# Shift of the exponentials by pairwise sums, the order of all instructions computed anew, and early loads into other places: an attention and MLP kernel

## The chip, the cores and the metric

The kernel runs on one core of a Trainium2 chip. The metric is the device time of one execution in microseconds (us). The five engines named below are PE (TensorE, the matrix engine), DVE (VectorE), ACT (ScalarE), POOL (GpSimd) and SP (SyncE, which here only issues DMAs). Each runs its own instructions strictly in its own order; between engines there are semaphores.

## The reference, cut to what matters

Random-feature attention for 8 batches of 8 heads (576 rows of 64), then a two-layer MLP over the 4608 tokens:

```
proj = x_s @ omega.T                      # x_s: q or k, scaled
h = proj - sum(x_s * x_s) / 2
phi = exp(h - max(h)) / sqrt(128)         # for q and for k
num = phi_q @ (phi_k.T @ v);  den = phi_q . sum(phi_k) + 1e-6
x = (num / den) as (4608, 512)
out = (silu-gate(x @ w_in)) @ w_out       # g = h * sigmoid(h)
```

So every row has one shift, `-(max - sq) - sq`, that is added to its 128 projections before the exponential.

## The kernel before, in words

Two heads make a pair; there are 32 pairs. Of a pair, PE projects k and q (`project`, L405, 16 small matmuls with 64 rows, and `project_mid`, L412, for the middle tile), DVE takes the row maxima from PSUM (`top`, L419 and L421), ACT squares k and q in their natural layout (`square`, L378), and DVE sums the squares (`square_sum`, L382). DVE then makes the shift in `shift` with two small instructions, a `tensor_tensor` (L425) and a `scalar_tensor_tensor` (L426), both with two operands in SBUF. ACT takes the exponentials (L441, or after an addition on DVE, L446 and L449, all at once in L455). PE sums the exponentials of k (L476 and L478 in the first eight pairs, later POOL adds them first, L461 to L466, and PE finishes, L470) and multiplies them with v (L499). DVE makes the denominators (`denom`, L487, ten products with a read each, and a reciprocal, L492), POOL scales with them (`normal`, L517), PE transposes (`turn`, L523), ACT copies (L535), PE multiplies (`numer`, L561). ACT and DVE split the result into a high and a low part (L580 and L585), which are the MLP's operand x.

The MLP runs as float32 in three passes over such high and low parts, with 512-column matmuls. The first 3 of 9 token tiles are done directly (`stage1` L736, `silu` L873 and L875, `g_low` L879, `stage2` L982); the other six in three pairs of tiles by a Strassen-like scheme: a first stage of products (L821, gathered by DVE on L868), and a second (L935, whose operands DVE prepares on L901 and L925). The weights are decoded from 64-bit words by ACT and DVE (L645, L659 to L665) and split by POOL (L678, L682); the first step of the MLP needs x of the first four pairs.

The order of all engines' instructions is computed in the kernel by a planner (`Plan.run`): a list of units of work, each with an engine, a duration, a due time (its key), predecessors, and places (rings of SBUF tiles and PSUM banks) that it takes and frees. The planner goes through the units by earliest possible start and then by key, and the kernel issues instructions in that order. `shift_keys` moves some keys by amounts drawn from the seeds in `SHIFTS`. Loads go on SP's queue in planned order. A load can be issued once its place is free: in the kernel before, `rawk`, `rawq`, `nat` and `v` are rings of two places each.

Of the kernel before, what the change touches and what calls it, by code (L numbers as in the profile page):

```python
# [19 lines left out]
P = 128  # L20
# [17 lines left out]
STRAIGHT_K = 22.298  # L38
STRAIGHT_Q = 25.574
# [3 lines left out]
WHOLE = ""  # L43
# [4 lines left out]
    "rawk": 2, "rawq": 2, "nat": 2, "v": 2, "sqk": 2, "sqq": 2, "hk": 2, "hq": 2,  # L48
# [6 lines left out]
for _f in range(16):  # L55
    RINGS[f"w{_f}"] = 1
PLAIN = 3
# [19 lines left out]
STAY = 19.283  # L77
HANDOFF = {"PE": 0.25, "ACT": 0.1, "DVE": 0.1, "POOL": 0.15, "SP": 0.2}
CALM = 0.5
SHIFTS = (  # L80
# [4 lines left out]
)  # L85
HOT = 100.0
PULSE = 0.24

# [10 lines left out]
PAIRS_22 = 52.068  # L99
PAIRS_28 = 85.000  # L100
# [6 lines left out]
PREPARE_2 = 0.176  # L107
LEAD_W = 14.593
# [49 lines left out]
def shift_keys(units):  # L158

    for seed in SHIFTS:  # L160
        r = random.Random(seed)
        part, wide = ((0.02, 6.0), (0.06, 3.0), (0.2, 1.5))[seed % 3]
        a, b = ((-20, 60), (40, 110), (100, 235), (200, 500), (420, 700), (640, 1100))[seed // 3 % 6]
        for u, d in [(u, r.gauss(0, wide)) for u in units if a <= u["key"] < b and r.random() < part]:
            u["key"] += d


class Plan:
# [6 lines left out]
    def add(self, name, eng, dur, key, fn, after=(), order=(), alloc=(), free=(), banks=0, table=None, lat=0.0, port=False, of="att", reads=()):  # L175
# [5 lines left out]
        self.units[name] = u  # L181
        for i in free:
            self.freed_by.setdefault(i, []).append(name)

    def run(self, until=None, heat=None):
        end, first = {}, {}
# [5 lines left out]
        table = None  # L192
# [10 lines left out]
        def slot_time(ring, back=0):  # L203
# [7 lines left out]
            for n in self.freed_by.get(s[i], ["never"]):  # L211
                if n not in end:
                    return None
                t = max(t, end[n] + HANDOFF[self.units[n]["eng"]])
            return t

        def bank_pools(u):
            pools = banks_of(u)
            chosen, when, used = [], 0.0, {p: 0 for p in pools}
            for _ in range(u["banks"]):  # L220
                best = None
                for p in pools:
                    t = slot_time(p, used[p])
                    if t is not None and (best is None or t < best[0]):
                        best = (t, p)
# [7 lines left out]
        while any(ready.values()):  # L233
            best = None
            for e, us in ready.items():
                pick, least = None, None
                for u in us:
                    t = 0.0
                    for a in u["after"]:
                        if self.units[a]["eng"] == e and not self.units[a]["lat"]:  # L240
                            t = max(t, end[a])
                        else:
                            t = max(t, first[a] + (CALM if e == "PE" and t > START_MLP else 0.0))
# [4 lines left out]
                    for j, (ring, _) in enumerate(u["alloc"]):  # L248
                        s = slot_time(ring, [r for r, _ in u["alloc"][:j]].count(ring))
# [12 lines left out]
                    t = max(t, free_at[e], port if u["port"] else 0.0)  # L262
                    key = u["key"]
                    if u["table"] and u["table"] != table:
                        key += STAY
                    least = t if least is None else min(least, t)
                    pick = (pick or []) + [(u, pools, key, t)]
                if not pick:
                    continue
                p = min((p for p in pick if p[3] <= least + 0.25), key=lambda p: p[2:])  # L270
# [6 lines left out]
            dur = u["dur"]  # L277
            if u["table"] and u["table"] != table:
                dur += SWITCH
                table = u["table"]  # L280
            if e == "PE":
                idle = t - free_at[e]
                u["hot"] = 0
                if u["banks"] and t < HOT and idle > 1.0:
                    since = max([free_at[e]] + [slot_time(p, pools[:i].count(p)) for i, p in enumerate(pools)])
                    u["hot"] = max(0, int((t - since - 0.4) / PULSE))
                    idle -= u["hot"] * PULSE
                if idle > 2.5:
                    warm = t + 4.0
                if t < warm:  # L290
                    dur *= 1.7
            free_at[e] = t + dur
            if u["port"]:
                port = t + dur
            done = t + dur
            if u["lat"]:
                pipe = max(pipe, t + dur + 1.0) + 0.75 * u["lat"]
                done = max(pipe + 0.25 * u["lat"], t + dur + 2.2)
            end[n] = done
            first[n] = done + HANDOFF[e]  # L300
            for i in u["reads"]:
                read[i] = e, first[n]
# [6 lines left out]
            if n == until:  # L309
                return t  # L310
# [9 lines left out]
def attention_mlp(ctx: ExitStack, tc: tile.TileContext, qT, kT, qn, kn, v, om_in, w_in, w_out, out, out_t):  # L320
# [43 lines left out]
    def load_raw(n, who):  # L364
        T["raw", n, who] = raw = new(f"raw{who}", [P, S + P])
        nc.sync.dma_start(raw, (kT if who == "k" else qT)[divmod(n, NPAIR)])

    def load_nat(n, who):
        T["nat", n, who] = nat = new("nat", [P, NC, D])
        nc.sync.dma_start(nat, (kn if who == "k" else qn)[divmod(n, NPAIR)])  # L370

    def load_v(n):
        T["v", n] = vt = new("v", [P, NC + 1, D])
# [5 lines left out]

    def square_sum(n, who):  # L380
# [3 lines left out]
    def raw_square(n, who):  # L384
        T["rsq", n, who] = sq = new({"k": "w12", "q": "w13"}[who], [P, S + P])
        nc.scalar.activation(sq, T["raw", n, who], AF.Square, scale=SCALE * 0.5**0.5)

    def mid_and_squares(n, who, ps):

        project_mid(n, who, ps)  # L390
# [1196 lines left out]
```

## Time and profile before

| | |
|---|---|
| three runs, us | 1018.7, 1022.9, 1023.67 (median 1022.9) |
| span of the profiled execution, us | 1018.3 (the page gives no other time of it) |
| busy: PE, DVE, ACT, POOL, us | 985.9, 779.8, 629.5, 362.0 |
| mean granted TensorE clock | 0.992 |
| chain that ended last | PE 73%, DVE 17%, DMA 4%, ACT 4% |

PE is busy for 97% of the span. Its matmuls are pipelined, so a busy PE isn't PE at its peak; start to start is the better measure of one. A group of instructions in the profile is named by line, engine, operation and tiles; what stands in square brackets in a timeline row is the idle time of the engine before the row and what ended it.

### The profile page before, as it was taken

How to read it: one execution, taken by the hardware profiler on the slowest of the kernel's cores; microseconds unless marked ns; L12 is line 12 of the kernel's file. 1: busy time of each engine (PE TensorE's matmuls, PEld its weight loads, DVE VectorE, ACT ScalarE, POOL GpSimd, SP SyncE). 2: the span in 40 equal slices, each digit the busy share in tenths (PEclk: the TensorE clock that was granted, in tenths of full speed). 3: DMA queues.
4: the chain of work that ended last, by engine and by line, in shares of the span. 5: the costliest groups of instructions: out<-in, count | busy, mean ns of one | idle time of the engine just before them, and what ended most of it. 6: DMA issues, size and time to landing. Idle time of an engine off the chain costs nothing.

```text
span 1018.3 us, 17380 instructions
## 1 busy us (share of the span) xinstructions
PE 985.9 (97%) x5784; PEld 787.9 (77%) x5784; DVE 779.8 (77%) x1898; ACT 629.5 (62%) x1229; POOL 362.0 (36%) x447
## 2 busy tenths in 40 slices
PE   8889999999999999999999999999999999999997
PEld 6767778777777777778878777777887877888886
DVE  6898897877776778798767799996458977546963
ACT  6778656655665666665888866667767444324551
POOL 2345464767577766573662202321020000000000
PEclk9899999999999999999999999999999999999999
DMA  8777566786767876667897577876445676555565
GB/s 303 254 226 264 191 244 222 241 285 219 229 212 228 275 236 220 214 216 285 315 308 235 187 226 240 269 242 214 166 157 177 224 262 227 189 196 195 187 215 156
DMA packets 107592, 232.94 MB, mean 229 GB/s; under 512 B 14704, under 2 KB 39408, under 8 KB 107504
## 3 DMA queue, kind: packets, MB, share of 16 engines
q1 hardware_dynamic: 107200, 231.52, 68.0%
q8 instruction: 46, 0.75, 0.3%
q10 hardware_dynamic: 304, 0.33, 0.1%
q14 instruction: 42, 0.34, 0.1%
HBM read 182.52 MB, written 49.28 MB: 228 GB/s over the span
## 4 chain that ended last, share of the span: by engine, by line
PE 73%; DVE 17%; DMA 4%; ACT 4%; issue 2%; POOL 0%; DVEq 0%; SPq 0%; ACTq 0%; POOLq 0%
PE ps_acc L821 18%; PE ps_acc L935 11%; PE ps_acc L982 10%; PE ps_h L736 9%; DVE prod L487 4%; PE ps_att L935 3%; DMA nat<-qn 3%; PE ps_att L405 2%; PE ps_att L821 2%; PE ps_h L821 2%; PE ps_h L935 2%; PE ps_att L499 1%; DVE w L925 1%; DVE mxq L421 1%; PE ps_fx L405 1%
## 5 line engine op out<-in xcount | busy, mean ns | idle before, releaser
L821 PE MATMUL ps_acc<-w,x 128*128 128x512 f32 x798 | 192.3, 394 | 1.4 <-DVE wo L868 1.2
L821 PEld LDWEIGHTS ps_acc<-w,x 128*128 128x128 f32 x798 | 147.3, 188 | 33.6 <-DVE wo L868 1.4
L517 POOL TENSOR_TENSOR hq<-hq,rd 128x384 f32<-128x384 f32 x96 | 83.0, 890 | 209.6 <-DVE rd L492 141.0
L736 PE MATMUL ps_h<-x,w 128*128 128x512 f32 x504 | 135.6, 404 | 2.1 <-POOL w L682 0.8
L982 PE MATMUL ps_acc<-wo,gh 128*128 128x512 f32 x384 | 122.8, 401 | 0.0
L935 PE MATMUL ps_acc<-w,x 128*128 128x512 f32 x456 | 115.9, 394 | 2.2 <-DVE w L925 2.0
L736 PEld LDWEIGHTS ps_h<-x,w 128*128 128x128 f32 x504 | 89.9, 188 | 22.5 <-ACT gf L875 1.7
L935 PEld LDWEIGHTS ps_acc<-w,x 128*128 128x128 f32 x456 | 84.2, 188 | 21.6 <-DVE w L925 3.9
L982 PEld LDWEIGHTS ps_acc<-wo,gh 128*128 128x128 f32 x384 | 69.0, 188 | 14.9
L935 PE MATMUL ps_acc<-gh,x 128*128 128x512 f32 x208 | 75.0, 397 | 3.4 <-DMA x<-wt 1.3
L982 PE MATMUL ps_acc<-wo,gl 128*128 128x512 f32 x192 | 75.2, 392 | 0.0
L378 ACT ACTIVATE nat<-nat 128x576 f32<-128x576 f32 x64 | 43.4, 690 | 28.3 <-DMA nat<-kn 16.6
L487 DVE CUSTOM_DVE_ANT_0 prod<-hq,ps_att 128x128 f32<-128x128 f32 (+1 forms) x160 | 45.9, 287 | 19.5 <-PE ps_att L507 8.7
L879 DVE TENSOR_TENSOR gl<-gf,gh 128x512 fp32r<-128x512 f32 x48 | 38.2, 798 | 18.1 <-ACT gf L875 18.1
L461 POOL TENSOR_TENSOR t<-hk 128x256 f32<-128x256 f32 x48 | 37.3, 798 | 39.4 <-ACT hk L455 31.5
L935 PEld LDWEIGHTS ps_acc<-gh,x 128*128 128x128 f32 x208 | 39.0, 188 | 14.0 <-ACT s L942 1.7
L873 ACT ACTIVATE gh<-ps_h 128x512 fp32r<-128x512 f32 x42 | 25.1, 599 | 39.3 <-PE ps_h L736 39.0
L982 PEld LDWEIGHTS ps_acc<-wo,gl 128*128 128x128 f32 x192 | 36.0, 188 | 8.0
L935 PE MATMUL ps_acc<-gl,x 128*128 128x512 f32 x104 | 40.8, 392 | 0.3 <-DVE gl L925 0.3
L466 POOL TENSOR_TENSOR es<-es,hk 64x128 f32<-64x128 f32 x48 | 27.1, 564 | 37.0 <-ACT hk L441 34.2
L535 ACT COPY en<-ps_att 128x384 f32<-128x384 f32 x46 | 22.0, 485 | 27.0 <-PE ps_att L523 26.9
L487 DVE CUSTOM_DVE_ANT_0 prod<-hq,ps_fx 128x128 f32<-128x128 f32 (+1 forms) x110 | 31.4, 286 | 9.1 <-ACT kw L512 3.3
(423 smaller groups left out, 2411.3 us busy)
## 6 DMA issues: line engine op xcount, KB each, us to landing
x<-ws SPq DMA_DIRECT2D x84, 512.0 KB, 3.3
x<-wt SPq DMA_DIRECT2D x48, 512.0 KB, 4.3
x<-wo_d SPq DMA_DIRECT2D x72, 256.0 KB, 3.3
wo<-wo_d SPq DMA_DIRECT2D x32, 512.0 KB, 4.0
rawk<-kT SPq DMA_DIRECT2D x32, 352.0 KB, 4.0
rawq<-qT SPq DMA_DIRECT2D x32, 352.0 KB, 4.7
v<-v SPq DMA_DIRECT2D x32, 320.0 KB, 4.8
nat<-kn SPq DMA_DIRECT2D x32, 288.0 KB, 4.3
```

The lines of the kernel that those rows point to most:

```text
L378: nc.scalar.activation(nat, nat, AF.Square, scale=SCALE * 0.5**0.5)
L405: nc.tensor.matmul(ps[:, i * M : (i + 1) * M], raw[r, o : o + P], oms[r], start=True, stop=True)
L461: nc.gpsimd.tensor_tensor(t[:, j], e[:, 5 * j : 5 * j + 2], e[:, 5 * j + 2 : 5 * j + 4], ALU.add)
L466: nc.gpsimd.tensor_tensor(es[r, j], es[r, j], e[r, MID], ALU.add)
L487: nc.vector.tensor_tensor_reduce(out=prod[r], in0=e[r, c], in1=z[r, j * M : (j + 1) * M], scale=1.0, scalar=GUARD, op0=ALU.mult, op1=ALU.a ...
L517: nc.gpsimd.tensor_tensor(e[:, c], e[:, c], rd[:, c].unsqueeze(2).broadcast_to([P, 3, M]), ALU.mult)
L736: nc.tensor.matmul(ph, w[:, i], x[:, j], start=k == 0 and n == 0, stop=k == NK - 1 and n == 2)
L821: nc.tensor.matmul(ph, ws[:, u, kk * P : (kk + 1) * P], o[:, x], start=i in (0, 1, 4) and kk == 0 and n == 0, stop=kk == 1 and n == 2, ski ...
L873: nc.scalar.activation(gh, ph, AF.Silu)
L879: nc.vector.tensor_tensor(gl, T.pop(("gf", t, f)), T["gh", t, f].bitcast(F32), ALU.subtract)
L935: nc.tensor.matmul(T["qb", p, chain][d], w[:, u, d * P : (d + 1) * P], x, start=i in (0, 1, 4) and s == 0 and n == 0, stop=s == NS - 1 and ...
L982: nc.tensor.matmul(T["po", t][j], g[:, js], w, start=f == 0 and n == 0, stop=f == NF - 1 and n == 2)
```

## The change

Three things are changed.

First, the maxima and the sums of squares are written side by side into one tile (`smk`, `smq`; 3 x 10 columns, three places each), the sums with a minus sign. `shift` is then two `tensor_reduce` additions over pairs of columns: `-(max + (-sq))`, and the sum of that with `-sq`. Each reads one operand. The values are the same.

Second, the planner's model has new numbers: occupation and duration per kind of unit (`COST`), times for changing the form of PE's matmuls (`ENTER`, `RESUME`), transfers (`MOVED`), shorter hand-over times, a smaller extra distance for PE (`CALM`, 0.5 to 0.1) and a new list of seeds with another rule for what a seed moves. With that the order of all engines changes. The number and kinds of instructions don't, but for 7 filling matmuls in place of 14.

Third, the loads of the second to fourth pair go into the places of weights that are decoded later (`HOMES`), where the first and the fifth pair keep the old ones.

```diff
-HANDOFF = {"PE": 0.25, "ACT": 0.1, "DVE": 0.1, "POOL": 0.15, "SP": 0.2}
-CALM = 0.5
+HANDOFF = {"PE": 0.053, "ACT": 0.034, "DVE": 0.034, "POOL": 0.075, "SP": 0.08}
+CALM = 0.1
+JOIN = 4.02
+ENTER = ((0.0, 0.0, 0.091, 0.091), (-0.08, 0.0, 0.093, 0.093), (0.097, 0.097, 0.0, 0.097), (0.1, 0.1, 0.1, 0.0))
+RESUME = (0.0, 0.1, 0.125, 0.135)
+HOMES = {("nat", 1, "k"): "w4", ("nat", 1, "q"): "w5", ("nat", 2, "k"): "w6", ("nat", 2, "q"): "w7"}
+HOMES |= {("nat", 3, "k"): "w8", ("nat", 3, "q"): "w9", ("raw", 2, "k"): "w10", ("raw", 2, "q"): "w11"}
+HOMES |= {("raw", 3, "k"): "w12", ("raw", 3, "q"): "w13", ("v", 2): "w14", ("v", 3): "w15"}
...
     def load_nat(n, who):
-        T["nat", n, who] = nat = new("nat", [P, NC, D])
+        T["nat", n, who] = nat = new(HOMES.get(("nat", n, who), "nat"), [P, NC, D])
...
     def square_sum(n, who):
-        T["sq", n, who] = s = new(f"sq{who}", [P, 10])
-        nc.vector.tensor_reduce(s[:, :NC], T.pop(("nat", n, who)), AX.X, ALU.add)
+        sums_at(n, who)
+        nc.vector.tensor_reduce(T["sm", n, who][:, 1, :NC], T.pop(("nat", n, who)), AX.X, ALU.add, negate=True)
...
     def shift(n, who, part):
-        m, s, nb = (part(T[a, n, who]) for a in ("mx", "sq", "nb"))
-        nc.vector.tensor_tensor(nb, m, s, ALU.subtract)
-        nc.vector.scalar_tensor_tensor(nb, nb, -1.0, s, ALU.mult, ALU.subtract)
+        sm = T["sm", n, who]
+        of, pairs = (part(sm[:, 2]), part(T["nb", n, who])), (sm[:, :2], sm[:, 1:])
+        for out, two, negate in zip(of, pairs, (True, False)):
+            nc.vector.tensor_reduce(out, part(two.rearrange("p k c -> p c k"), True), AX.X, ALU.add, negate=negate)
```

On SP, the loads after the first four, in the kernel before (`rawk`, `rawq` are the projected layout, `nat` the natural one, `wraw` raw weights):

```order
L374 DMA v<-v 128x640 x2
L366 DMA rawq<-qT 128x704
L366 DMA rawk<-kT 128x704
L638 DMA wraw<-w_in 128x512
L638 DMA wraw<-w_out 128x512
L638 DMA wraw<-w_in 128x512
L366 DMA rawk<-kT 128x704
L370 DMA nat<-kn 128x576
L366 DMA rawq<-qT 128x704
L370 DMA nat<-qn 128x576
```

and now (a load into `w_...` is one of a second to fourth pair):

```order
L474 DMA rawk<-kT 128x704
L474 DMA rawq<-qT 128x704
L478 DMA w_191<-kn 128x576
L478 DMA w_193<-qn 128x576
L482 DMA v<-v 128x640
L474 DMA w_209<-qT 128x704
L474 DMA w_212<-kT 128x704
L478 DMA w_218<-kn 128x576
L478 DMA w_220<-qn 128x576
L482 DMA w_235<-v 128x640
L474 DMA w_239<-kT 128x704
L738 DMA wraw<-w_in 128x512
```

The first weights have moved from the place behind eight loads of pairs to one behind seventeen, and the second pair's natural layouts from behind the weights to a place ahead of them.

On ACT, the first pair's exponentials and what follows them, in the kernel before (`nat` rows are squares, `wre` the weights' exponents):

```order
L378 ACTIVATE nat<-nat 128x576 x2
L441 ACTIVATE hk<-ps_att,nbk 128x128 x4
L441 ACTIVATE hk<-ps_fx,nbk 128x128 x4
L441 ACTIVATE hk<-ps_acc,nbk 128x128
L441 ACTIVATE hq<-ps_acc,nbq 128x128 x9
L645 ACTIVATE wre<-wraw 128x512 x2
L504 COPY kt<-ps_acc 128x128
L378 ACTIVATE nat<-nat 128x576
```

and now:

```order
L541 ACTIVATE hk<-ps_att,nbk 128x128 x4
L541 ACTIVATE hq<-ps_acc,nbq 128x128
L541 ACTIVATE hk<-ps_att,nbk 128x128 x4
L541 ACTIVATE hk<-ps_fx,nbk 128x128
L541 ACTIVATE hq<-ps_acc,nbq 128x128 x8
L486 ACTIVATE w_191<-w_191 128x576
L486 ACTIVATE w_193<-w_193 128x576
L486 ACTIVATE w_218<-w_218 128x576
L604 COPY kt<-ps_fx 128x128
```

The weights' exponents have left this place, the squares of the second and third pair follow the exponentials directly, and one exponential of q stands among those of k.

On PE, between the sum over k of the thirteenth pair (L470, now L570, just ahead of these rows) and the transposes of its q (L523, now L623, the last row), in the kernel before:

```order
L736 MATMUL ps_h<-x_2009,w_1915 128x512 x3
L736 MATMUL ps_h<-x_2290,w_1915 128x512 x3
L982 MATMUL ps_acc<-wo,gh 128x512 x2
L982 MATMUL ps_acc<-wo,gl 128x512
L982 MATMUL ps_acc<-wo,gh 128x512 x2
L982 MATMUL ps_acc<-wo,gl 128x512
L736 MATMUL ps_h<-x_1234,w_1993 128x512 x3
L736 MATMUL ps_h<-x_1614,w_1993 128x512 x3
L412 MATMUL ps_att<-oms,rawk 128x128
L523 MATMUL ps_att<-ident,hq 128x128 x3
```

and now:

```order
L836 MATMUL ps_h<-x_1283,w_1756 128x512 x3
L836 MATMUL ps_h<-x_1580,w_1756 128x512 x3
L836 MATMUL ps_h<-x_1971,w_1756 128x512 x3
L836 MATMUL ps_h<-x_2252,w_1756 128x512 x3
L836 MATMUL ps_fx<-x_1283,w_1894 128x512 x3
L836 MATMUL ps_fx<-x_1580,w_1894 128x512 x3
L836 MATMUL ps_fx<-x_1971,w_1894 128x512 x3
L836 MATMUL ps_fx<-x_2252,w_1894 128x512 x3
L503 MATMUL ps_att<-oms,rawk 128x128 x8
L509 MATMUL ps_fx<-oms,rawk 128x128
L623 MATMUL ps_fx<-ident,hq 128x128 x3
```

Twenty-four matmuls of 512 columns stand together now where eighteen in two mixed groups stood, and a projection has come between them and the transposes.

## Rows read from the trace of the kernel before

**Rows 1.** Windows: us, length, busy time and count by engine, clock, DMA share, GB/s.
```profile
0.00:57.60 57.60, 48.03 (x408) 40.47 (x409) 45.76 (x144) 39.86 (x116) 18.44 (x28) 0.88 0.80 278
...
83.00:1013.00 930.00, 915.96 (x5213) 731.50 (x5212) 709.64 (x1680) 570.19 (x1064) 331.86 (x406) 1.00 0.68 228
...
578.00:690.00 112.00, 107.67 (x621) 85.05 (x617) 107.42 (x237) 72.68 (x169) 29.32 (x32) 1.00 0.72 237
...
140.00:160.00 20.00, 17.66 (x93) 14.63 (x92) 17.88 (x33) 14.31 (x32) 9.09 (x9) 0.91 0.61 199
```

**Rows 2.** Timeline of DVE, 6 to 77 us: start, us, instruction, idle before.
```profile
6.53 0.69 DVE L421 TENSOR_REDUCE mxk<-ps_fx 128x4 f32<-128x512 f32 x1 [5.52 <-PE ps_fx L405]
...
8.99 1.28 DVE L421 TENSOR_REDUCE mxq<-ps_acc 128x4 f32<-128x512 f32 x2
...
14.39 0.29 DVE L487 CUSTOM_DVE_ANT_0 prod<-hq,ps_fx 128x128 f32<-128x128 f32 x1 [0.18 <-PE ps_fx L478]
...
17.99 0.22 DVE L492 RECIPROCAL rd<-den 128x9 f32<-128x9 f32 x1
...
27.18 0.69 DVE L585 TENSOR_TENSOR x<-ps_fx,x 128x512 fp32r<-128x512 f32 x1 [0.29 <-ACT x L580]
...
76.34 0.67 DVE L585 TENSOR_TENSOR x<-ps_acc,x 128x512 fp32r<-128x512 f32 x1
```

**Rows 3.** Timeline of PE, 75 to 78 us.
```profile
75.77 0.47 PE L736 MATMUL ps_h<-x,w 128*128 128x512 f32 x1
77.07 0.73 PE L736 MATMUL ps_h<-x,w 128*128 128x512 f32 x2 [0.82 <-DVE x L585]
```

**Rows 4.** Groups of DVE's weight decoding: shapes, count, busy us, mean ns, idle before.
```profile
L661 DVE SCALAR_TENSOR_TENSOR w<-wre,w 128x512 uint32<-128x512 uint32 x32 | 26.6, 832 | 3.2 <-ACT wre L645 2.4
...
L665 DVE SCALAR_TENSOR_TENSOR w<-wraw,w 128x512 uint32<-128x512 uint32 x32 | 24.6, 770 | 0.9
```

**Rows 5.** Timeline of ACT, 9 to 18 us.
```profile
9.18 1.14 ACT L441 ACTIVATE hk<-ps_att,nbk 128x128 f32<-128x128 f32 x4 [0.68 <-DVE nbk L426]
...
11.64 2.44 ACT L441 ACTIVATE hq<-ps_acc,nbq 128x128 f32<-128x128 f32 x9
...
17.57 0.68 ACT L378 ACTIVATE nat<-nat 128x576 f32<-128x576 f32 x1 [1.78 <-DMA nat<-kn]
```

**Rows 6.** Timeline of PE, 306 to 311 us.
```profile
306.02 0.39 PE L982 MATMUL ps_acc<-wo,gl 128*128 128x512 f32 x1
306.34 1.31 PE L499 MATMUL ps_fx<-hk,v 128*64 128x128 f32 x20
...
308.56 1.66 PE L736 MATMUL ps_h<-x,w 128*128 128x512 f32 x6
310.05 0.59 PE L470 MATMUL ps_att<-es,ones 128*128 128x256 f32 x2
```

**Rows 7.** By line on DVE: count, ns min/median/max, first to last start.
```profile
L425 DVE TENSOR_TENSOR nbq<-mxq,sqq x60: 142/161/1261, 11.2 to 765.6; 128x8 f32<-128x8 f32 x28, 128x1 f32<-128x1 f32 x28, 128x9 f32<-128x9 f32 x4
...
L426 DVE SCALAR_TENSOR_TENSOR nbq<-nbq,sqq x60: 158/170/1221, 11.4 to 765.8; 128x8 f32<-128x8 f32 x28, 128x1 f32<-128x1 f32 x28, 128x9 f32<-128x9 f32 x4
...
L382 DVE TENSOR_REDUCE sqk<-nat x32: 736/744/754, 7.1 to 685.8; 128x9 f32<-128x576 f32 x32
...
L419 DVE TENSOR_REDUCE mxk<-ps_att x18: 276/281/292, 34.3 to 757.1; 128x1 f32<-128x128 f32 x18
```

**Rows 8.** Windows as in rows 1, of lines L425 and L426 alone, DVE.
```profile
578.00:690.00 112.00, 2.92 (x14) 1.00 0.72 237
...
578.00:690.00 112.00, 2.74 (x14) 1.00 0.72 237
```

**Rows 9.** Waits of PE's weight loads: us in total, times, longest.
```profile
PEld ps_fx L523 <- POOL hq L517: 5.2, 6, 0.9
```

**Rows 10.** Timeline of PE, two single waits.
```profile
152.97 0.52 PE L523 MATMUL ps_fx<-ident,hq 128*128 128x128 f32 x3 [2.04 <-issue]
...
619.19 1.43 PE L935 MATMUL ps_acc<-w,x 128*128 128x512 f32 x5 [1.07 <-DVE w L925]
```

More of the change, by code (lines that the diff above doesn't have):

```diff
@@ L87 @@
 PULSE = 0.24
+IDLE = 1.0
 def clock(step):
@@ L158, in shift_keys @@
 def shift_keys(units):
+    units = list(units)
     for seed in SHIFTS:
         r = random.Random(seed)
[L162 to L165, printed above, removed]
+        how = seed % 5
+        a = r.uniform(-30, 1010)
+        b = a + r.choice((30, 60, 120, 250, 1100))
+        here = [u for u in units if a <= u["key"] < b]
+        if how < 3 and here:
+            part, wide = ((0.02, 6.0), (0.06, 3.0), (0.2, 1.5))[how]
+            for u in r.sample(here, int(part * len(here)) + 1):
+                u["key"] += r.gauss(0, wide)
+        elif here:
+            like, d = r.choice(here)["name"], r.gauss(0, 3.0)
+            for u in here:
+                if u["name"][0] == like[0] if how == 3 else u["name"][1:2] == like[1:2]:
+                    u["key"] += d
 class Plan:
@@ L181, in add, with cost, run @@
         self.units[name] = u
+        kind = name if isinstance(name, str) else name[0]
+        u["occ"], u["took"] = self.cost(u)
+        u["form"] = FORMS.get(kind, 1) if eng == "PE" else 0
+        u["moved"] = (MOVED.get(kind, 0.74) if eng == "SP" else 0.4) if lat else 0.0
         for i in free:
             self.freed_by.setdefault(i, []).append(name)
-    def run(self, until=None, heat=None):
-        end, first = {}, {}
+    def cost(self, u):
+        n, e = u["name"], u["eng"]
+        kind = n if isinstance(n, str) else n[0]
+        if e == "SP":
+            return 0.75 if kind == "gt" else 0.42, 0.4
+        if kind == "z":
+            return (2.22, 2.4) if n[1] < DIRECT else (0.32, 0.594) if n[1] == DIRECT else (0.538, 0.702)
+        if kind == "m2":
+            return COST["m"] if u["dur"] > 1 else COST["s1"]
+        if kind == "exp":
+            return (0.26, 0.37) if n[3] == 2 else (1.0, 1.16)
+        if kind == "top":
+            return (0.2, 0.28) if n[3] == 2 else (0.6, 0.685)
+        if kind == "low":
+            return (0.27, 0.35) if n[3] == 2 else (0.605, 0.69)
+        if kind == "wd" and n[-1] == 0:
+            return 0.34, 0.42
+        if kind in COST:
+            return COST[kind]
+        if e == "POOL":
+            return (1.28, 1.29) if kind == "ol" else (1.23, 1.28) if u["dur"] > 1 else (0.69, 0.74)
+        return (0.4, 0.4) if e == "ACT" else (0.605, 0.69)
+    def run(self):
+        end = {}
         port, warm = 0.0, 0.0
@@ L239, in run @@
                     for a in u["after"]:
-                        if self.units[a]["eng"] == e and not self.units[a]["lat"]:
-                            t = max(t, end[a])
+                        if self.units[a]["eng"] == e and e != "SP":
+                            if e in ("ACT", "DVE"):
+                                t = max(t, end[a] + AGAIN)
                         else:
-                            t = max(t, first[a] + (CALM if e == "PE" and t > START_MLP else 0.0))
+                            t = max(t, end[a] + HANDOFF[e] + (CALM if e == "PE" and t > START_MLP else 0.0))
                     for i in u["reads"]:
@@ L290, in run @@
                 if t < warm:
-                    dur *= 1.7
-            free_at[e] = t + dur
+                    occ, took = occ * 1.7, took * 1.7
+                form = u["form"]
+            free_at[e] = t + occ
             if u["port"]:
[L294 to L300, printed above, removed]
+                port = t + (0.7 if n[0] == "sums" else occ)
+            end[n] = t + took
+            if u["moved"]:
+                pipe = max(t + FIRST_BYTE, pipe) + u["moved"]
+                end[n] = pipe + LANDING
             for i in u["reads"]:
-                read[i] = e, first[n]
+                read[i] = e, end[n] + AGAIN
             for ring, i in u["alloc"]:
@@ L1108, in attention_mlp @@
         if not merged:
[L1109 removed]
+            add(("kv", n), "PE", 1.2, at(n, 6.5, 28.5), lambda ps, n=n: kv(n, ps), after=e["k"] + [("v", n)], order=[("kv", n - 1)] if n else [], banks=1,
                 free=[("v", n), ("h", n, "k")])
```

153 lines of the change are left out of this document (78 added, 75 removed), and 54 rows, old and new, of tables (RINGS, SHIFTS).

## The prediction

> **What bounds the kernel now.** I read the windows by stage first, then DVE's timeline up to 77 us, then the list of waits, then the places on PE's timeline where it stands still. PE does the work of the span, and three stretches differ.
>
> In the first 57.6 us PE is busy 48.0, partly at a granted clock of 0.88, and DVE 45.8 [rows 1]. Here DVE is what everything waits for: its first maximum starts at 6.53, and the first MLP operand is split at 27.18 and the fourth at 76.34, after a nearly unbroken row of work [rows 2]. The MLP's first step needs all four: PE has begun on the fourth at 75.77 with its high part and stands until 77.07, when DVE delivers the low part [rows 3].
>
> From 83 to 1013 us PE is busy 915.96 of 930, so 14.0 us of standing are left to be won there, of which some 1.8 lie in 140 to 160 beside a clock of 0.91 [rows 1]. The waits are single ones: transposes that wait for POOL's scaling, six times and 5.2 in all, 0.9 at most [rows 9], and places like 2.04 before a transpose at 152.97 and 1.07 before a product at 619.19 [rows 10]. From 578 to 690 DVE is busy 107.4 of 112 us and PE 107.7 [rows 1]: two engines at their limit.
>
> **The change part by part.** All sums are against the profiled execution's span, 1018.3 us; the median of the runs is 4.6 above it, which I carry over.
>
> *The start.* I walk DVE through the new order. Prices: a maximum over four tiles 0.6 (two take 1.28, one alone 0.69), the denominators of a pair 3.6 (14.39 to 17.99) [rows 2], a sum of squares 0.74 (0.66 start to start, as the maxima overlap too), a maximum of one tile 0.28 [rows 7], 0.2 where it overlaps, the second and third words of a weight 0.83 and 0.77 [rows 4], which holds their waits for POOL too, and for the first word an estimate of half of that. The first pair's shifts are done at 11.45, the second pair's k maxima at 12.85. Then DVE waits: ACT has 18 exponentials ahead of the second pair's squares. They took 4.9 in the old order (9.18 to 14.08 [rows 5]); now they start at 9.7, lose 0.75 to one q exponential that stands among the k ones, and end at 15.3, so the first square ends at 15.9. That is 3.0 us of DVE. Then sums and shifts to 17.6, first denominators to 21.1, the second pair's q, two sums and one weight to 26.5, second denominators to 30.0, first operand split at 30.1: later than 27.18, but with 20 more denominator products done. From there nothing that I can find in the two orders stops DVE for long: third denominators from 40.4 to 43.9, second operand at 43.9, third at 56.6, fourth pair's exponentials of q done by ACT at 60.9 (1.1 us of DVE's waiting), its denominators to 64.5, then scaling, transposes, copies and the product to 69.3, high part, low part: the fourth operand is split from 70.1 to 70.7, against 77.0 before. That is 6.3 earlier. What was cheapened: ahead of that operand the new order has one sum, one single maximum and two first, one second and two third words of weights less, 3.0 to 3.8 us of DVE work that comes later, beside PE's MLP. PE itself has one projection, one middle tile and six transposes less behind it, fifteen small matmuls at 0.11 (ten take 1.31 with the last one's latency [rows 6]), 1.7 us, and keeps 6.3 - 1.7 = 4.6. I take 4.3, since a halved clock can come with either gap. Bounds: without any wait but the first, DVE's sum ends the fourth operand at 66.9, so 8.2 won; with as much waiting as before (12.9) and the 3.0 of ACT on top, at 75.8, so 0.5 lost.
>
> *The loads.* They enable that order and cost nothing by themselves: the natural layout of the second pair's k held ACT for 1.78 until 17.57 [rows 5] and is now ahead of all weights. The first weight now comes behind seventeen loads of 0.29 to 0.36 MB each (by their shapes), 5.6 MB, which at 278 GB/s [rows 1] land at about 20 us; DVE wants it at 24. Were that cover gone, each us would be a us of the start.
>
> *The form of PE's matmuls.* By the two orders the changes between forms fall from 373 to 349. Going from 512 columns into the small k-times-v matmuls costs 0.09 (306.02 to 306.34 is 0.32, a matmul 0.227), coming back 0.13 (308.56 to 310.05 for six) [rows 6]; but eighteen of the twenty-four are into or out of small matmuls of full rows and columns, where I take no gap. What counts is four returns and two changes among small forms: 4 x 0.13 + 2 x 0.1, 0.7, and with the slower first matmul behind a return 0.8 won, of 0 to 2.4 (all of them at 0.1).
>
> *The shift.* The two old instructions have medians of 161 and 170 ns and reach 1261 and 1221, while sums over one operand stay within 736 and 754 [rows 7]. A reduction of 16 elements is not in the trace; the nearest are 281 ns for 128 elements from PSUM and 744 for 576 [rows 7], and the line through both gives 166 at 16. From below it is 0.08 (half a median), from above 0.28. DVE's total falls a lot, but only where DVE is the limit does it count: from 578 to 690 there are 28 such instructions of 0.20 [rows 8], so 28 x 0.035 = 1.0 won, 3.4 at the lower price, 2.2 lost at the upper. I take 0.7, as in the walk the chain is hardly changed (0.4 in the first 57 us).
>
> The Trainium skill speaks on both sides. "VectorE: DVE Perf Modes" (Rules for kernel authors) calls `tensor_reduce` on a hot path the slowest operation and advises another form; by it the upper price would hold and the sum would be 2.9 worse. "SBUF — State Buffer" (Who interferes with whom) says that two operands in SBUF contend with POOL's reads and that `tensor_reduce` on this chip never does; the rows agree with that one, a spread of 18 ns against one of 1100 [rows 7], and by it the stretch above the medians goes.
>
> *The order after 83 us.* Nothing in the amounts changes: at the end of the first three tiles, of the products and of each second stage, the two orders have within one pair the same attention done. So only the 14.0 us of waits are open. For transposes behind POOL the chain is denominators 3.6, one scaling 0.8 and the way in and out, about 5.5. Counted at 0.23 for a matmul of 512 columns and 0.07 to 0.22 for a small one, of the tenth to twenty-first pair the old order put 5.0 to 5.7 us of PE work between the sum and the first transpose, all twelve at the edge; the new one puts 4.3 to 8.4, four at 5.0 or less, six at 6.4 or more. That is 1.0 won of 5.2 [rows 9]. The other waits, some 9, are each one place where a chain was a little late; the places are re-drawn, and I let two thirds come again elsewhere, since PE's distance to its suppliers is planned shorter. Won 3.0, together 4.0; from 10 won to 6 lost (the third rival). A wait for a load near the end stays: the last sixty DMAs on SP stand as they did.
>
> Sum: 4.3 + 0.8 + 0.7 + 4.0 = 9.8. So a span of 1008.5 instead of 1018.3, and 1013.1 at the median: **1013**.
>
> **The rivals.**
>
> *Nearly all waits go.* The start reaches its bound (8.2), and of the 14.0 us 9 go: 8.2 + 0.8 + 0.7 + 9 = 18.7, 1004. For it: all twelve transposes at the edge in the old order point to a planner that saw no cost there. Against it: four of them are still at 5.0 or less.
>
> *The start gives nothing.* DVE's work is the same in sum, its waits only change place (3.0 for squares, and then the halved clock), and loads that come early bring nothing that waited on them. Then 0 + 0.8 + 0 + 2 = 2.8 and 1020, within what can't be told from no change. For it: DVE waited for a load hardly at all before; against it: ACT did, and the walk.
>
> *Slower: the first second stage is bound by DVE.* Between DVE's last gathering of the first products and its last output of that stage the new order has 4 maxima, one set of denominators, two sums of squares and 5 operand preparations more, and 6 operand sums and remainders fewer: 2.4 + 3.6 + 1.4 - 0.7 = 6.7 us at the 0.6 to 0.7 of one. Only 4.6 of 112 us are free on DVE [rows 1], and each set of denominators holds it 3.6 in one piece, which can cost PE something like the 1.07 before 619.19 [rows 10]. It decides from the point where those 4.6 are used up. With reductions at the upper price (2.2) and the start 0.5 lost, less 0.8 for forms: 6.7 + 2.2 + 0.5 - 0.8 = 8.6 lost, 1031.
>
> **How the numbers follow.** A half per cent, 5.1 us, is what a measurement here can tell from no change. My forecast has 0.50 (its own range 1007 to 1018), the first rival 0.17, the second 0.25, the third 0.08. Faster by more than 5.1 (under 1017.8): 0.47 + 0.17 = 0.64. Within: 0.03 + 0.24 + 0.01 = 0.28. Slower: 0.08. The range reaches over most of the first and second rivals: 1001 to 1022.
>
> **What would show it.** In the new profile: shift instructions near 0.17 with no long ones (up to 1.2) among them; DVE's fourth split near 70.5 and PE's MLP without a stop around it, with about 3 us of DVE idle near 13 to 16 until ACT's squares; PE's busy share from 83 on above 98.5%; DVE's share from 578 to 690 no higher than 96%. The forecast is wrong if the fourth split is later than 75, if PE's waits after 83 us add up to 14 or more, or if DVE fills the first second stage and PE stands there for more than 6 us.

## The result, and the profile after

The changed kernel takes 1027.89 us (1026.36 to 1029.54), 1.0066 of the kernel before, with an interval of 1.0043 to 1.0088: slower by 0.7%, above the range that was given. The profiled execution's span is 1027.4 instead of 1018.3.

The windows of the changed kernel, as in [rows 1]; the last one is new here.

```profile
0.00:57.60 57.60, 44.33 (x404) 37.04 (x404) 44.88 (x143) 39.49 (x115) 19.11 (x28) 0.94 0.76 269
...
83.00:1013.00 930.00, 912.20 (x5163) 726.30 (x5162) 687.01 (x1676) 563.19 (x1054) 332.88 (x406) 0.99 0.69 226
...
578.00:690.00 112.00, 104.94 (x600) 82.94 (x598) 104.43 (x245) 68.48 (x166) 28.08 (x30) 0.97 0.68 221
...
140.00:160.00 20.00, 19.94 (x120) 15.54 (x121) 14.84 (x30) 17.14 (x35) 10.78 (x10) 1.00 0.74 246
...
440.00:700.00 260.00, 249.36 (x1456) 197.80 (x1455) 204.76 (x510) 169.48 (x358) 84.57 (x106) 0.99 0.71 234
```

The last of these windows in the kernel before:

```profile
440.00:700.00 260.00, 255.67 (x1543) 203.56 (x1541) 220.45 (x561) 188.31 (x378) 92.87 (x120) 1.00 0.75 252
```

PE's stand of 2.04 at 152.97 is gone with its window's gap. But from 83 to 1013 PE now stands 17.8 us, more than the 14.0 of before, and 10.6 of these lie in 440 to 700, where before had 4.3; there PE runs 87 matmuls fewer. From 578 to 690 PE stands 7.1 while DVE is busy 3.0 us less than before [rows 1]: DVE, busy 93% of that stretch, isn't the engine that is full.

DVE's timeline at the start, to be held against [rows 2], and PE's around the fourth operand, against [rows 3]:

```profile
15.28 0.75 DVE L495 TENSOR_REDUCE smk<-w 128x9 f32<-128x576 f32 x1 [2.96 <-ACT w L486]
...
30.45 0.64 DVE L685 TENSOR_TENSOR x<-ps_acc,x 128x512 fp32r<-128x512 f32 x1
...
70.58 0.68 DVE L685 TENSOR_TENSOR x<-ps_acc,x 128x512 fp32r<-128x512 f32 x1
```

```profile
70.55 0.50 PE L836 MATMUL ps_h<-x,w 128*128 128x512 f32 x1
71.31 0.73 PE L836 MATMUL ps_h<-x,w 128*128 128x512 f32 x2 [0.25 <-DVE x L685]
```

The walk through DVE's work came out: 2.96 of waiting for ACT's squares (3.0 forecast), first split at 30.45 (30.1), fourth at 70.58 (70.1). The start is earlier as the walk said; what became of that comes below.

The shift's two instructions by line, against [rows 7]: count, ns min/median/max, first to last start.

```profile
L524 DVE TENSOR_REDUCE smk<-smk x60: 141/158/174, 8.7 to 786.4; 128x8 f32<-128x16 f32 x28, 128x1 f32<-128x2 f32 x28, 128x9 f32<-128x18 f32 x4
...
L524 DVE TENSOR_REDUCE nbq<-smq x60: 154/171/176, 10.7 to 796.1; 128x8 f32<-128x16 f32 x28, 128x1 f32<-128x2 f32 x28, 128x9 f32<-128x18 f32 x4
```

The medians are those of the pair that went, and the long ones are gone. Added up over all 240 shift instructions of a trace: 73.1 us before, with 70 of them over 0.3, and 39.3 now, with none.

The waits of PE and of its weight loads from 83 to 1013 us: line waited for, us in total, times, longest.

```profile
PE ps_att L503 <- ACT hq L541: 3.5, 1, 3.5
...
PE ps_acc L1035 <- DVE w L1025: 1.7, 2, 1.3
...
PE ps_att L623 <- POOL w L782: 1.5, 1, 1.5
...
PEld ps_att L623 <- POOL hq L617: 0.9, 2, 0.5
```

The last row is the only one of weight loads that wait for POOL's scaling in this stretch. In the kernel before there is none: all six of [rows 9] lie ahead of 83 us, which the prediction overlooked. The first row is the largest single stand. The timeline of its neighbourhood, all engines:

```profile
642.00 0.29 DVE L587 CUSTOM_DVE_ANT_0 prod<-hq,ps_att 128x128 f32<-128x128 f32 x1 [1.60 <-ACT kw L612]
...
645.71 3.56 POOL L617 TENSOR_TENSOR hq<-hq,rd 128x384 f32<-128x384 f32 x3 [19.48 <-DVE rd L592]
...
646.02 1.31 DVE L1025 TENSOR_TENSOR gl<-w,gh 128x512 fp32r<-128x512 f32 x1
647.26 4.84 DVE L730 TENSOR_TENSOR w<-x,w 128x512 fp32r<-128x512 f32 x4
...
653.88 0.68 DVE L518 TENSOR_REDUCE smq<-ps_h 128x4 f32<-128x512 f32 x1
...
655.40 0.17 DVE L524 TENSOR_REDUCE nbq<-smq 128x8 f32<-128x16 f32 x1
655.67 1.14 ACT L541 ACTIVATE hq<-ps_att,nbq 128x128 f32<-128x128 f32 x4 [3.88 <-DVE nbq L524]
...
656.86 2.84 PE L503 MATMUL ps_att<-oms,rawk 64*128 64x128 f32 x16 [3.47 <-ACT hq L541]
```

Read from the top: denominators start 1.60 late, behind an ACT copy. Their end lets POOL's three scalings start just when DVE does its remainders. These have two operands in SBUF, and five of them, among POOL's work, take 1.2 to 1.3 instead of some 0.6, while POOL's scalings take 1.19 each instead of the 0.83 of undisturbed ones (the last section shows why). DVE comes to the maxima of the next q late, then the shift, then ACT's exponentials, and PE stands 3.47 for the PSUM place that these read. After that the granted clock falls, to 0.66 over these 10 us, which costs 3.4 us of full clock:

```profile
655.00:665.00 10.00, 8.14 (x35) 6.81 (x36) 7.88 (x19) 5.29 (x16) 0.91 (x2) 0.66 0.41 140
```

### The profile page after: what moved, and what is told of

It is laid out like the page before. It is cut to its first block, busy times and chain, and to the rows that moved or that the text cites. A ratio compares the mean times of both kernels' runs of the same rounds, so it can differ in the third digit from the quotient of the medians.

```text
span 1027.4 us, 17292 instructions
## 1 busy us (share of the span) xinstructions
PE 989.0 (96%) x5770; PEld 788.0 (77%) x5770; DVE 757.2 (74%) x1898; ACT 624.4 (61%) x1227; POOL 365.7 (36%) x447
## 4 chain that ended last, share of the span: by engine, by line
PE 62%; DVE 17%; ACT 7%; DMA 6%; POOL 4%; issue 4%; SPq 0%; POOLq 0%; ACTq 0%; DVEq 0%
PE ps_acc L921 12%; PE ps_acc L1035 10%; PE ps_acc L1082 8%; PE ps_h L836 8%; DVE prod L587 3%; PE ps_att L1035 3%; PE ps_h L921 2%; PE ps_att L503 2%; PE ps_fx L921 2%; PE ps_att L921 2%; DVE w L1025 2%; DMA nat<-qn 2%; ACT hq L541 2%; PE ps_fx L1035 2%; PE ps_fx L836 1%
## 5 line engine op out<-in xcount | busy, mean ns | idle before, releaser
L921 PE MATMUL ps_acc<-w,x 128*128 128x512 f32 x738 | 177.6, 395 | 1.6 <-ACT wo L954 1.4
L617 POOL TENSOR_TENSOR hq<-hq,rd 128x384 f32<-128x384 f32 x96 | 87.0, 933 | 219.1 <-DVE rd L592 203.7
L921 PEld LDWEIGHTS ps_acc<-w,x 128*128 128x128 f32 x738 | 136.5, 188 | 32.8 <-ACT wo L954 2.3
L836 PE MATMUL ps_h<-x,w 128*128 128x512 f32 x480 | 127.4, 405 | 4.0 <-POOL w L778 1.2
L1035 PE MATMUL ps_acc<-w,x 128*128 128x512 f32 x456 | 116.8, 396 | 1.7 <-DVE w L1025 1.7
L836 PEld LDWEIGHTS ps_h<-x,w 128*128 128x128 f32 x480 | 87.6, 190 | 26.4 <-ACT gf L975 2.8
L1035 PEld LDWEIGHTS ps_acc<-w,x 128*128 128x128 f32 x456 | 84.3, 188 | 21.8 <-DVE w L1025 3.6
L587 DVE CUSTOM_DVE_ANT_0 prod<-hq,ps_att 128x128 f32<-128x128 f32 (+1 forms) x190 | 54.4, 286 | 15.4 <-ACT kw L612 9.1
L486 ACT ACTIVATE nat<-nat 128x576 f32<-128x576 f32 x58 | 39.8, 694 | 20.2 <-DMA nat<-kn 11.1
L566 POOL TENSOR_TENSOR es<-es,hk 64x128 f32<-64x128 f32 x48 | 25.0, 521 | 55.7 <-ACT hk L541 53.0
L635 ACT COPY en<-ps_att 128x384 f32<-128x384 f32 x54 | 26.1, 487 | 29.7 <-PE ps_att L623 25.9
L878 POOL TENSOR_TENSOR wraw<-w,wraw 128x256 fp32r<-128x256 f32 x32 | 23.5, 735 | 33.8 <-ACT wraw L876 33.4
```

The source lines that it names most:

```text
L486: nc.scalar.activation(nat, nat, AF.Square, scale=SCALE * 0.5**0.5)
L566: nc.gpsimd.tensor_tensor(es[r, j], es[r, j], e[r, MID], ALU.add)
L587: nc.vector.tensor_tensor_reduce(out=prod[r], in0=e[r, c], in1=z[r, j * M : (j + 1) * M], scale=1.0, scalar=GUARD, op0=ALU.mult, op1=ALU.a ...
L617: nc.gpsimd.tensor_tensor(e[:, c], e[:, c], rd[:, c].unsqueeze(2).broadcast_to([P, 3, M]), ALU.mult)
L635: nc.scalar.copy(T["en", n][:, 3 * g * P : 3 * (g + 1) * P], T.pop(("t", n, g)))
L836: nc.tensor.matmul(ph, w[:, i], x[:, j], start=k == 0 and n == 0, stop=k == NK - 1 and n == 2)
```

## The experiments

Three theories stood at first. **A**: the loss is that one place. **B**: the new shift itself costs. **C**: the new order leaves less time between a supplier and PE in many places, so that each small lateness reaches PE. The work that PE still has while a supplier is late is called the order's cover here. All ratios are to the kernel before, and the us behind them are the difference from 1 times 1022.4.

**e1_old_shift** keeps the new order and puts the old shift back:

```diff
-    of, pairs = (part(sm[:, 2]), part(T["nb", n, who])), (sm[:, :2], sm[:, 1:])
-    for out, two, negate in zip(of, pairs, (True, False)):
-        nc.vector.tensor_reduce(out, part(two.rearrange("p k c -> p c k"), True), AX.X, ALU.add, negate=negate)
+    m, s, nb = part(sm[:, 0]), part(sm[:, 1]), part(T["nb", n, who])
+    nc.vector.tensor_tensor(nb, m, s, ALU.add)
+    nc.vector.scalar_tensor_tensor(nb, nb, -1.0, s, ALU.mult, ALU.add)
```

> The changed kernel in its own order, with the old shift put back (an addition and a scalar_tensor_tensor, two operands in SBUF each). Theory A (the loss is in the new order, the new shift is a small help): slower than the changed kernel by 0.5 to 4 us, as 57 of the 120 shifts stand beside POOL's work, where the old pair had a median of 0.99 us instead of 0.35, and most of that is hidden: 1028.5 to 1032. Theory B (the new shift itself costs, by its form): faster than the changed kernel by 3 us or more, 1025 or less.

1050.29 us, 1.0285 [1.0265, 1.0306]. The shift by line in its trace:

```profile
L523 DVE TENSOR_TENSOR nbq<-smq x60: 150/188/1233, 11.1 to 816.3; 128x8 f32<-128x8 f32 x28, 128x1 f32<-128x1 f32 x28, 128x9 f32<-128x9 f32 x4
...
L524 DVE SCALAR_TENSOR_TENSOR nbq<-nbq,smq x60: 159/169/1219, 11.3 to 816.5; 128x8 f32<-128x8 f32 x28, 128x1 f32<-128x1 f32 x28, 128x9 f32<-128x9 f32 x4
```

The long ones are back (79 of 240 over 0.3, 80.2 us in all). Neither number that was expected came. B falls: in this order the new shift is worth 22 us. A's number falls too, by some 20.

**e2_new_shift** is the kernel before, its order untouched, with the reductions in place of the pair.

> The kernel before in its own order, with only the new shift (pairwise sums with one operand). Theory A: 0.5 to 2.5 us faster than the kernel before, 1020 to 1022, since 37 of the 120 shifts go from 0.99 to 0.38 us beside POOL, mostly hidden. Theory B (the new shift costs): 3 us or more slower, 1025 or more.

1014.11 us, 0.9927 [0.9909, 0.9945]: 7.5 won, three times the most that A said and the other way from B. The shift instructions sum to 39.0 us in its trace. So the same 34 us of DVE's work buy 7.5 in the old order, and 41 buy 22 in the new one. And with the same shift the new order is 14 us longer than the old.

**e3_maxima_first** and **e4_load_aside** take the place at 653 apart from both ends: e3 puts the maxima and the shift ahead of three of the four remainders on DVE, e4 puts the ACT copy that stands behind a late load after the copy and the square that the denominators need. `ahead` takes the named units out of the order and puts them just before the unit named last. Of e3:

```diff
+    todo = plan.run()
+    todo = ahead(todo, [('ssum', 30, 'q'), ('ql', 0, 5, 1), ('ql', 0, 5, 2), ('ol', 1, 1, 1), ('ol', 1, 1, 0), ('ol', 1, 0, 0)], ('ql', 0, 5, 3))
```

and of e4:

```diff
+    todo = plan.run()
+    todo = ahead(todo, [('oh', 1, 1, 0)], ('oh', 1, 1, 1))
```

> The changed kernel with one edit in DVE's order: the two maxima and the shift of the 29th pair's q go ahead of three of the four operand remainders (and of a sum of squares and two remainders) that stand before them at 648.5 us. Theory A (one place: these maxima come 4.4 us late behind remainders that take 1.22 to 1.31 us beside POOL, PE stands 3.5 us at 653 and runs at the lower clock until 661): the stand and the low clock go, 5 to 6 us, 1022 to 1023. Theory C (the order is short of slack everywhere, what is saved at one place is lost at the next): less than 2 us, 1026 or more.

> The changed kernel with one edit in ACT's order: the copy that waits 1.6 us for a late load at 639 (it lands 5.1 us after its issue) goes behind the small copy and the square that stood behind it. Theory A (DVE beside POOL makes the lateness, the load only adds 1.6 to it): the stand at 653 shrinks from 3.5 to about 1.9 us, 1.6 us won, or up to 4 if the clock stays up: 1024 to 1026. Theory D (the late load is the origin): the stand and the low clock go, 1022 or less.

1028.58 us, 1.0075 [1.0051, 1.0099], and 1027.76 us, 1.0066 [1.0047, 1.0084]: both as the change itself. PE's timeline at the place, in e3 and in e4:

```profile
654.14 1.16 PE L503 MATMUL ps_att<-oms,rawk 64*128 64x128 f32 x14 [1.82 <-ACT en L635]
```

```profile
658.08 0.48 PE L503 MATMUL ps_att<-oms,rawk 64*128 64x128 f32 x2 [2.00 <-ACT hq L541]
```

The stand shrinks by 1.5 or more in each, PE stands 7.8 and 8.3 us from 440 to 700 instead of 10.6, and the mean clock from 640 to 680 is 0.96 in both instead of 0.91. The time doesn't follow, so A's number doesn't come. But the two edits take away only about half of what that place costs, 3.47 of standing and 3.4 of clock, and the 3 us in question are hardly more than the intervals; where they went isn't shown. What settles that A isn't the whole is e6, below: more than a third of the loss lies ahead of 440.

**e5_new_start** and **e6_new_to_440** are hybrids. The order is a table; e5 has the new one up to 91 us and the old one behind it, e6 the new one up to 440. Both have the new shift. Like e2 and all later kernels they have four places for the shift's tiles instead of three; DVE alone writes and reads these, so no other engine holds one.

```diff
-        for u in plan.run():
+        for u in in_table_order(plan.units.values()):
```

> The changed kernel's order up to 91 us (by the planner's time), then the order of the kernel before for all that is left; the new shift throughout, and the loads in their new places. Theory E (the new order is good in its start, 3 to 5 us as forecast, and loses later): 2 to 5 us faster than the old order with the new shift (1014.1), so 1009 to 1012. Theory F (the start gives nothing that lasts; what PE has early it loses at the next DVE-bound place): 1013 or more.

> The changed kernel's order up to 440 us (by the planner's time), then the order of the kernel before; the new shift throughout. Theory C (the new order loses against the old one wherever DVE is late, and most of it behind 440: from 440 to 700 the changed kernel loses 11.4 us against the kernel before, the old order with the new shift none): 10 to 12 us faster than the changed kernel, 1016 to 1018. Theory G (the loss behind 440 is caused by lateness brought along from the stages ahead of it): less than 5 us, 1023 or more.

1014.05 us, 0.9937 [0.9922, 0.9952], and 1019.47 us, 0.9990 [0.9980, 1.0000]. e5 against e2: the new start is worth nothing by times (0.1%, inside the intervals). e5 and e6 against the changed kernel part the order's 14 us: 5.4 for 91 to 440 (0.9990 - 0.9937), 7.8 behind 440 (1.0066 - 0.9990). For e5 theory F's number came. e6 won 7.8 back from the changed kernel (8.4 by the medians), less than C's 10 to 12 and more than G's 5. The windows of e6 and of e2:

```profile
440.00:700.00 260.00, 256.46 (x1527) 204.49 (x1526) 206.78 (x536) 181.57 (x366) 87.50 (x109) 1.00 0.74 244
```

```profile
440.00:700.00 260.00, 256.11 (x1540) 203.91 (x1537) 213.94 (x557) 187.27 (x381) 92.87 (x119) 1.00 0.75 249
```

PE stands 3.5 and 3.9 there. e6 enters the window in the changed kernel's state and doesn't lose in it, so the loss there is the order's of that stretch, not something carried in.

This table counts PE's work up to a point of before from the matmuls on record (those of 512 columns 0.228 us each, small ones 0.11) and says how much later each kernel has started the same amount:

| at (us of before) | changed | e1 | e2 | e5 | e6 | e8 | e10 |
|---|---|---|---|---|---|---|---|
| 80 | -3.8 | +1.9 | +1.4 | -2.1 | -3.7 | -2.6 | +0.7 |
| 440 | -2.6 | +14.6 | -4.5 | -6.6 | -2.7 | -13.1 | +0.2 |
| 700 | +8.8 | +28.2 | -4.7 | -6.4 | -3.2 | -17.8 | -0.3 |
| 1000 | +9.1 | +29.9 | -5.0 | -4.6 | -1.6 | -23.0 | -2.3 |

Each row is one execution: that of before was the fastest of its runs and that of e2 the slowest of its six, so e2's -5.0 stands for 7.5 by times. The weights of the small matmuls and the order within a stretch leave an entry open by some 1.6 us. The changed kernel is 3 to 4 ahead after the start, and loses 11 or more between 440 and 700; of these 6.3 are more standing (10.6 against 4.3), and 3.4 the clock. e2, which has nothing from the start, wins 5.9 between 80 and 440.

**What makes an order touchy?** The planner has DVE's work on two operands in SBUF and POOL's work begin only one behind the other, each with its undisturbed time. In the trace their rows overlap and are longer, since the row of the one that comes second holds its wait; POOL waits for DVE too, unlike what the next expectation says (last section). If C holds, an order planned with such lateness must be faster, without any other edit. So orders were searched by moving single units and keeping a move if the planner's sum for the order fell, with two allowances: **beside POOL** (POOL starts at once, a DVE instruction with two operands counts about twice while beside it, POOL 1.45 times: the length of the rows, not the turns behind it) and **late** (durations vary by 3 to 4%, loads come late). e7_replanned starts from e5's order, e8_replanned_old from the old one; both have the new shift.

> The changed kernel's instructions (new shift, new places of loads) in an order worked out anew: from the order of the run with the new start, single instructions are moved as long as the sum of the planner's durations falls, but with three things taken from the traces: DVE's work on two operands in SBUF takes twice as long while POOL works (1.2 to 1.3 us for 0.605), POOL doesn't wait for it, and every duration and load is also tried some per cent late. Theory C (what was lost is the cover that an order has against DVE being late): such an order is faster than both kernels and than the old order with the new shift, 1000 to 1009. Theory I (the old order is as good as an order gets here, since PE's matmuls and the start set the rest): 1012 or more.

> As the run before this one, but worked out from the kernel before's whole order, its start included. Theory C: 1003 to 1012, slower than the other by the start, 0 to 4 us. Theory I: 1014, as the old order with the new shift.

e7: 1008.74 us, 0.9884 [0.9866, 0.9902]. **e8: 996.77 us, 0.9766 [0.9748, 0.9785]**: it beats both kernels, by 2.3% and 3.0%. e7 lies where C said; e8 is faster than C's 1003 to 1012, and 12 us ahead of e7, where it was to be slower by what the new start wins. Its windows and its waits, of PE from 83 to 1013:

```profile
83.00:440.00 357.00, 356.63 (x2306) 283.14 (x2305) 272.92 (x789) 233.63 (x425) 238.72 (x281) 1.00 0.73 243
440.00:700.00 260.00, 259.39 (x1547) 207.41 (x1547) 206.00 (x539) 181.37 (x374) 86.10 (x115) 1.00 0.77 255
```

```profile
PE ps_h L615 <- ACT en L741: 0.5, 1, 0.5
PE ps_fx L676 <- POOL es L672: 0.2, 1, 0.2
PE ps_acc L1141 <- issue: 0.2, 1, 0.2
```

PE stands 1.0 in 617 us. The clashes haven't gone: DVE's two-operand instructions over 0.85 us are 55 in e8, 55 in before, 63 in e2 and 49 in the changed kernel, and what they take over 0.69 adds up to 27.8, 25.6, 31.1 and 25.6 us. About as many, about as dear; what differs is how long PE stands, which fits C: in e8 PE mostly has work until they are over.

Three controls. **e10_no_allowance** is the same search from the same start with neither allowance, **e11_beside_pool_alone** and **e12_late_alone** with one each.

> The same moving of single instructions from the kernel before's order as in the fastest run, with the new shift, but with the planner's durations as they stand: no allowance for DVE's work beside POOL, none for being late. By those durations it is the shortest of all orders tried, 6 us shorter than the one of 996.8. Theory C (fitting an order to durations without allowance uses up its cover, as in the change): 1005 to 1020, at least 8 us slower than the one of 996.8. Theory J (any such fitting from the old order is good, and the change's order only started from a bad place): 1000 or less.

> As the run before this one, but with the one allowance that DVE's work on two operands in SBUF takes twice as long beside POOL; no lateness otherwise. Theory C in its narrow form (POOL beside DVE is what the change's planner lacks): 995 to 1000. In its wide form (it is any lateness, loads too): 1002 to 1010.

> As the two runs before this one, but with lateness alone: four sets of durations that vary by 3 to 4% and loads that come up to some 60% late, and no allowance for POOL. Narrow form of theory C: 1003 to 1012. Wide form: 995 to 1002.

e10: 1021.15 us, 0.9998 [0.9983, 1.0013]. e11: 1004.05 us, 0.9828 [0.9805, 0.9851]. e12: 1014.97 us, 0.9930 [0.9911, 0.9949]. By the planner's undisturbed times e10's is a shorter order than e8's; on the chip it is 24 us longer, and longer than e2, the order that the search started from. (The new places of the loads, which e2 hasn't, stand in e5 too and cost 1.0 at most together with the new start.) Its window and its waits:

```profile
440.00:700.00 260.00, 256.86 (x1542) 202.80 (x1541) 213.29 (x560) 176.65 (x371) 94.37 (x118) 1.00 0.72 246
```

```profile
PE ps_fx L729 <- DVE smk L630: 2.3, 1, 2.3
...
PE ps_h L942 <- ACT gf L1081: 2.2, 2, 1.3
...
PE ps_acc L1141 <- ACT s L1148: 1.8, 2, 1.2
```

An order made shorter on durations without any allowance loses 7 us of time, as C has it, and 1 us more than C's range. Against e2, most of the gain comes with the clashes (e11, 10 us), lateness alone brings nothing that can be told from e2 (e12), and both together 16. Against e10, which is the same search without either, the clashes are worth 17, lateness 7 and both 24, so lateness does count: it makes good what the bare search loses. Neither form of C foresaw this pair: e11 came where the wide form had it (1002 to 1010), e12 slower than both. Each kind of order was drawn once, so the 6 between e11 and e8 may hold some chance.

**e9_replanned_old_shift** is e8's order with e1's edit. C was read as: an order with cover pays little for the old shift, 3 to 10 us. The rival, **K**, said 15 or more.

> The fastest order so far (worked out from the order of the kernel before, 996.8 us) with the old shift put back. Theory C (what counts is the cover that an order has): it pays less for the 22 to 24 us that DVE is busy longer than the changed kernel's order does, which paid 22 us: 3 to 10 us, 1000 to 1007. Theory K (every order that is faster than the old one is as sensitive): 15 us or more, 1012 or more.

1013.35 us, 0.9918 [0.9901, 0.9935]: 15.5 more than e8 by the ratios. C in this form falls, and K's number came: per us that DVE is busy longer, e8's order pays 0.37, the changed one 0.55, the old one 0.22. A reading that fits is that e8's cover was laid out for the cheap shift and 42 us more on DVE use it up; that isn't shown. Only the old order, planned with the old shift's durations, takes the difference at 7.5.

## Why the prediction was wrong

By its own terms, measured by the chain before → e2 → e5 → e6 → changed:

| term | forecast | measured |
|---|---|---|
| shift | -0.7 | -7.5 (e2) |
| start, loads with it | -4.3 | +1.0, none within the intervals (e2 to e5) |
| order behind the start, forms with it | -4.8 | +13.2 (e5 to changed) |
| sum | -9.8 | +6.7 |

- **The step that failed** is that of the order after 83 us: "Nothing in the amounts changes ... So only the 14.0 us of waits are open", with two thirds of the waits let back in, and a bound of 6 lost. It counted the waits that were there and could go. It didn't ask how many suppliers that were in time in the old order would be late in the new one. The order behind 91 us costs 13, and e5 and e6 place it: 5.4 from 91 to 440 and 7.8 behind 440. Two of the prediction's own signs of being wrong are in the trace: 17.8 us of standing after 83 us (14 or more), and 7.1 from 578 to 690 (more than 6), though with DVE not full. That it is suppliers without cover is C, which e8 and e10 to e12 support and e9 limits.
- **The step that mis-sized** is the shift. The new price was right, but it was counted from 578 to 690 alone, against the 0.20 of that stretch [rows 8], "only where DVE is the limit". Only 3 of the 70 long ones lie there; 63 lie from 83 to 578, where DVE is not full, and over all 240 the mean was 0.30, not 0.20. [rows 7] had them in sight: 1261 beside a median of 161. So the gain was in the tail, 34 us of DVE's work, and it was worth 7.5 where the prediction put 0.7: a DVE with 23% of its time free isn't free where PE waits for it.
- **The start** was walked right and priced wrong. The trace shows 3 to 4 of the 4.3, but no us of it is in the times of e5 against e2. The start also differs from one execution to the next: the trace of e4, which has the changed kernel's start, is 0.8 ahead at 80 us or less, since PE there waits 1.5 for a first load instead of 0.5 and DVE is late with it. The clock, which the prediction feared in taking 4.3 for 4.6, doesn't tell the two apart: over the first 57.6 us it is 0.91 in e4 and 0.94 in the changed kernel, but 0.91 also in e6, which is as far ahead as the changed kernel. By the table e5's lead over e2 is 3.5 at 80, 2.1 at 440 and 1.7 at 700, and gone at 1000; what takes it behind 700 isn't shown.
- **The rival "slower"** came near in time (1031 against 1028) and in part in place, since PE stood 7.1 in 578 to 690. Its mechanism was wrong: DVE had not more work there but less, 104.43 instead of 107.42 [rows 1].
- **Reductions of 16 elements** take 158 to 172 at the median. The value drawn through two longer ones, 166, was right. The upper price, with the warning of the Trainium skill ("VectorE: DVE Perf Modes", Rules for kernel authors) beside it, isn't seen in any of the 240. The other page of the Trainium skill ("SBUF — State Buffer", Who interferes with whom), by which this operation never contends, agrees with the trace: 131 of the 240 overlap an instruction of POOL, and the longest takes 176 ns.
- **Transposes behind POOL**, where 1.0 was to be won of 5.2, were misread. The list was taken over the whole span, and all six waits [rows 9] lie in the first 83 us. Behind it there was nothing to win; the changed kernel has 0.9 there. The margins that were counted for the tenth to twenty-first pair had nothing to do with those six.
- **The forms of the matmuls** (0.8) weren't measured alone.
- **Two rows were read inexactly**, without weight for the sum: from 140 to 160 PE stands 2.34, not 1.8 [rows 1], and it is twenty small matmuls, not ten, that take 1.31 [rows 6].

Open stays which rule of the planner makes the difference. One candidate shows in the traces: from 440 to 700, 17% of the changed kernel's PE units take their PSUM place within 0.2 us of its last read's end, against 6% before, 4% in e2 and e8, 5% in e6 (counted from the ends of the reads and the starts of the matmuls). Counted for the two kinds of place that have one buffer each (`ps_h`, `ps_fx`), it is 9 of 56 units here against 2 of 58 before; but from 83 to 440, where the new order loses too, it is 15 of 94 against 18 of 98, so this mark can't be the whole. The planner's allowance for that hand-over was cut in the change, and so was PE's extra distance (`CALM`); neither was tried alone.

## What to carry to other kernels

Price an edit on an engine that is not the bound over the whole kernel, by its longest cases and its mean, not by its median or one stretch, and then ask what the order pays per us of its lateness: here 0.22, 0.37 and 0.55 in three orders. A search fitted to durations without their spread, and without the waits that engines make for each other, lost 7 us here, and with both it won 16; a planner should be given the durations as the trace has them beside other work. To judge a new order, freeze it as a table and swap it stage by stage with the old one: that shows in two runs what mending single stands didn't.

## What was not expected of the hardware

DVE and POOL take turns, one whole instruction at a time, when DVE reads two operands from SBUF. The changed kernel at the place above, and a shift instruction of the kernel before:

```profile
645.71 1.09 POOL L617 TENSOR_TENSOR hq<-hq,rd 128x384 f32<-128x384 f32 x1 [19.48 <-DVE rd L592]
646.02 1.31 DVE L1025 TENSOR_TENSOR gl<-w,gh 128x512 fp32r<-128x512 f32 x1
646.75 1.27 POOL L617 TENSOR_TENSOR hq<-hq,rd 128x384 f32<-128x384 f32 x1
647.26 1.31 DVE L730 TENSOR_TENSOR w<-x,w 128x512 fp32r<-128x512 f32 x1
```

```profile
79.96 1.28 POOL L682 TENSOR_TENSOR w<-w,w 128x512 fp32r<-128x512 f32 x1
80.04 1.22 DVE L426 SCALAR_TENSOR_TENSOR nbq<-nbq,sqq 128x8 f32<-128x8 f32 x1
```

POOL's first scaling ends at 646.80, DVE's instruction about 0.55 behind it, POOL's second 0.69 behind that, and so on; undisturbed they take 0.68 and 0.83. On DVE this holds for every long one: each `tensor_tensor` of 128x512 on two SBUF operands that takes over 0.85 us (38 in before, 40 in the changed kernel, 49 in e2, 41 in e8) ends 0.54 to 0.56 us behind the end of an instruction of POOL. All 70 shift instructions over 0.3 us in before, 79 in e1 and 87 in e9, of one to nine elements per partition, end within 0.04 us behind one: they wait out the rest of POOL's instruction, up to 1.26 us for work of 0.16. So a clash costs what is left of the other engine's instruction, which depends on when the two meet, and the median doesn't show it. Instructions of 128x512 that read one operand from PSUM stayed within 0.70 in all the traces, and the shift's reductions within 0.18. Longer durations for such pairs in the search, as a stand-in for the turns, were worth 17 us (e10 to e11) of 1021, without one instruction more or less.
